# Attention weights of 20 pairs turned by VectorE and DMAs instead of TensorE, in a fused attention and feed-forward kernel

## The chip, the cores and the metric

One core of a Trainium2 chip runs the whole program in one launch. The metric is the device time of one execution in microseconds (us), as the median of several runs. TensorE is called PE (its matmuls) and PEld (its weight loads, which overlap the matmuls), VectorE is DVE, ScalarE is ACT, GpSimd is POOL and SyncE is SP. DMAs can be started from the queues of SP and of ACT.

## The reference

q, k and v are [8 batches, 8 heads, 576 positions, 64], all float32. For each of the 64 heads two attentions are computed and added:

- pooled: q, k and v are averaged over groups of 4 positions, which leaves 144; softmax attention over the 144, and each of the 144 results is repeated 4 times;
- local: softmax attention in which position i sees only the positions j with |i - j| < 4.

```
out_up    = repeat(softmax(q_d k_d^T / 8) v_d, 4)
out_local = softmax(where(|i-j| < 4, q k^T / 8, -1e9)) v
x = (out_up + out_local), heads side by side      # [4608 tokens, 512]
h = x @ w_in                                      # [4608, 2048]
g = h if h >= 1, 0 if h <= -1, else (h + 1)^2 / 4
out = g @ w_out                                   # [4608, 512]
```

## The kernel before

**Numbers in two parts.** The feed-forward products run in a float32 form of reduced precision (fp32r). Each operand is held as a high and a low part (`xh`, `xl` for x; `gh`, `gl` for g; two halves of each weight tile), and each product is the sum of three matmuls.

**Pairs, chunks, steps.** Two heads that lie side by side make a pair; there are 32 pairs, four to a batch. The tokens go through the feed-forward part in 11 chunks: one of 512, eight of 384, two of 512. In the first stage (the order written out in `ORDER`, lines 97 to 142) PE works on pairs 0 to 7 and on chunk 0. In the last stage the last two chunks go through a scheme with fewer products (`strassen`). Between them lies the middle stage, the loop of lines 1176 to 1216. Each of its steps n runs `mm1`, 12 matmuls of 384 columns that make one 128-row slice of h (line 858), and `mm2`, 9 matmuls of 512 columns that take up the slice of g from two steps before (line 921). Between the two, on ACT, DVE and POOL, lies the gate: ACT copies the slice out of its one PSUM bank (`m`, line 879), so that the next `mm1` can write there, DVE and ACT form g (lines 883 to 889), ACT rounds it (`gh`, 896), POOL takes the rest (`gl`, 902). At the end of each chunk ACT copies three output banks to `osb` (line 945), and SP's queue stores them (line 946).

**Joins.** The attention of pairs 8 to 31 is joined into the middle stage: `JOINS` (line 149) lists the 25 steps at which a join stands. The join of pair n does, right behind `mm1` of its step, the value products of pair n - 1 and the scores of pair n, in one stretch of small matmuls: the pooled values (line 633, which read the weights `ap`), the local scores in windows of 64 positions (651), the pooled scores (619), and last the local values (675, which read the weights `al`). Then DVE, POOL and ACT take maxima, exponentials and sums (lines 695 to 737), DVE adds up x of pair n - 1 (717), and `split` copies it to `xh` on ACT (581) and takes the rest to `xl` on POOL (582). In the next step DVE sums, inverts and multiplies (743 to 746 the local weights `sl`; 247 and 254, in `normalise`, the pooled weights `sp`, with a second copy `sp_rest` of the last 16 keys). The weights then lie with the queries on the partitions, and the value products need the keys there. From pair 10 on three DMAs of SP copy them to fresh tiles (759 to 762), so that they can be read as fp32r. One more step later PE turns them with 11 transposes of 128 by 128: five for the local weights (776), six for the pooled ones (779). ACT copies both out of PSUM to `ap` and `al` (784, 789). `al` is not needed before the end of the next join, which stands three to seven steps behind.

**What sets the order.** Each engine works through its own queue in a fixed order. A planner puts the instructions of the middle stage in order when the program is built; `tc.keep_in_program_order` ties PE's, `tc.issue_after(x)` puts a block's instructions behind x on x's engine, and `tc.high_priority` lets the gate go first. Tiles with one tag share one buffer: `x` and `ap` share one, `al` and `local` another, `vp` and `pooled` a third, and a writer waits until the readers of the tile before are done.

Of the kernel before, what the change touches and what calls it, by code (L numbers as in the profile page):

```python
# [10 lines left out]
F32 = mybir.dt.float32  # L11
# [35 lines left out]
WIN = 64  # L47
# [2 lines left out]
OUT_LEN = [61, 58, 58, 58, 53, 58, 58, 58, 58, 56]  # L50
NB = len(WIN_START)
NG = NB // 2

# [95 lines left out]
JOINS = [17, 20, 23, 26, 30, 37, 44, 51, 58, 63, 68, 73, 78, 85, 92, 99, 106, 111, 115, 120, 125]  # L149
JOINS += [131, 135, 138, 142]  # L150
assert len(JOINS) == NALL - SECOND + 1


class Rotation:
# [10 lines left out]
def attention_then_ffn(ctx: ExitStack, tc, qT, kT, vw, vp, vq, members, w_in, w_out, out):  # L165
# [24 lines left out]
    def load(n, name):  # L190

        if n == len(pairs):
            return
        b, p = pairs[n]
        if name in "qk" and n < NPAIR:
            t = wpool.tile([P, 1024], F32, name=f"first_{name}{n}", tag=f"w{'i' if name == 'q' else 'o'}{NFC - NPAIR + n}")
            source = (qT if name == "q" else kT)[b, p]
            queue = nc.scalar if name == "q" and n == 0 else nc.sync
            for c0, c1 in ((0, HALF), (HALF, S)) if n == 0 else ((0, S),):
                queue.dma_start(t[:, c0:c1], source[:, c0:c1])  # L200
        elif name in "qk":
# [395 lines left out]
    def pooled_sums(n):  # L597

        pooled_sum("q")
        pooled_sum("k")  # L600

    def join(n, pool):

        scores = pool.tile([P, 2, 512], F32, name="score_ps", tag="ga")
# [10 lines left out]
        def pooled_scores(i):  # L615
            for h in range(2):
                hs = slice(h * D, (h + 1) * D)
                x = h if i < 2 else 1 - h
                put(nc.tensor.matmul(
                    sp_v[i][x * D : (x + 1) * D, :],  # L620
                    state["qd"][hs, i * QB : i * QB + D],
                    state["kd"][hs, :],
                    start=True,
                    stop=True,
                    skip_group_check=True,
                ))

        def pooled_values(main):
            ap, vd = state["ap"], state["vd"]
            for h in range(2):  # L630
                hs = slice(h * D, (h + 1) * D)
                ks = slice(0, P) if main else slice((1 - h) * D, (2 - h) * D)
                put(nc.tensor.matmul(
                    pp_v[hs, :],
                    vd[ks, hs] if main else vd[ks, P : P + D],
                    ap[ks, 0 if main else 1, :, h, :],
                    start=main,
                    stop=not main,
                    skip_group_check=True,
                ))  # L640
# [3 lines left out]
        if n < NALL:  # L644
            q, k = loaded["q"], loaded["k"]
            for g in range(NG):
                for h, s in ((0, 0), (1, 1), (1, 0), (0, 1)):
                    x = h ^ s
                    w = WIN_START[x * NG + g]
                    hs = slice(h * D, (h + 1) * D)  # L650
                    put(nc.tensor.matmul(
                        sl_v[x * WIN : (x + 1) * WIN, s, g * WIN : (g + 1) * WIN],
                        q[hs, w : w + WIN],
                        k[hs, w : w + WIN],
                        start=True,
                        stop=True,
                        skip_group_check=True,
                    ))
            pooled_scores(0)
        if n > SECOND:  # L660
            pooled_values(False)
        if n < NALL:
            pooled_scores(2)
            pooled_scores(1)
        if n > SECOND:
            al, v = state["al"], loaded["v"]
            for g in range(NG):
                for r, h in ((0, 0), (1, 0), (0, 1), (1, 1)):
                    s = r ^ h
                    hs = slice(h * D, (h + 1) * D)  # L670
                    rs = slice(s * WIN, (s + 1) * WIN)
                    i = r * NG + g
                    o = OUT_START[i]
# [39 lines left out]
        if n > SECOND:  # L713
            x = apool.tile([P, S], F32, name="x", tag="ap", bufs=1)
            xd = apool.tile([P, SD], F32, name="xd", tag="kd", bufs=1)
            nc.vector.tensor_scalar_mul(xd, pp_v, 1.0 / FACTOR)
            nc.vector.tensor_tensor(
                x.rearrange("p (a s f) -> p a s f", a=2, f=FACTOR),
                pl_v.rearrange("p a (s f) -> p a s f", f=FACTOR),
                xd.rearrange("p (a s) -> p a s", a=2).unsqueeze(3).broadcast_to(  # L720
                    [P, 2, SD // 2, FACTOR]
                ),
                op=ALU.add,
            )
        if n == SECOND + 1:
            yield
        if n < NALL:
            nc.scalar.activation(slf, slf, AF.Exp, scale=0.125)  # L728
            for j, i in enumerate((0, 2, 1)):
# [5 lines left out]
                    scale=scale,  # L735
                    accum_out=sums[:, NB + i : NB + i + 1],
                )
        if n > SECOND:
            split(n - 1, x)
        if n == NALL:  # L740
            return
        yield
        nc.vector.tensor_reduce(sums[:, 0:NB], slf, axis=AX.X, op=ALU.add)
        nc.vector.tensor_scalar_add(scales, sums, 1e-9)
        nc.vector.reciprocal(scales, scales)
        nc.vector.tensor_tensor(
            slf, slf, scales[:, 0:NB].unsqueeze(2).broadcast_to([P, NB, WIN]), op=ALU.mult
        )
        normalised = normalise(sp, scales)
        vpt = loaded["vp"]  # L750
        vd = apool.tile([P, P + D], F32, name="vd", tag="vd", bufs=1)
        state["vd"] = vd
        with tc.issue_after(shifted.ins):
            nc.gpsimd.tensor_tensor(vpt[:, 0:2, :], vpt[:, 0:2, :], vpt[:, 2:4, :], op=ALU.add)
            nc.gpsimd.tensor_tensor(vd, vpt[:, 0, :], vpt[:, 1, :], op=ALU.add)
        moved = n > SECOND + 1
        if moved:
            local = apool.tile([P, NG * P], F32, name="local", tag="al", bufs=1)
# [175 lines left out]
    def result(c, t):  # L934

        osb = temp("osb", F32, "osb")
        rows = out[CHUNKS[c][0] : CHUNKS[c][0] + CHUNKS[c][1], :].rearrange("(a b) d -> b a d", a=2)
        rows = rows[t * P // 2 : (t + 1) * P // 2]
        if c == LATE + 1 and t == 2:
            nc.vector.tensor_copy(osb[:, 0:256], places["o"](t)[:, 0:256])  # L940
            nc.scalar.copy(osb[:, 256:], places["o"](t)[:, 256:])  # L941
            nc.sync.dma_start(rows[:, :, 0:256], osb[:, 0:256])
            nc.scalar.dma_start(rows[:, :, 256:], osb[:, 256:])
        else:
            nc.scalar.copy(osb, places["o"](t))  # L945
            nc.sync.dma_start(rows, osb)
        done("osb")

    def mm2(c, f):
# [368 lines left out]
```

## Time and profile before

| | |
|---|---|
| time, median of 3 runs | 886.82 us (886.55 to 886.97) |
| time of the profiled execution | 887.74 us |
| its span, from the first to the last instruction | 885.9 us |
| PE, PEld busy | 99%, 90% |
| DVE, ACT, POOL busy | 62%, 52%, 42% |
| granted TensorE clock | 1.000 of full speed |
| HBM, read and written | 101 GB/s over the span |

The profile is one execution. A row of the timeline gives the start and the duration of an instruction; PE's matmuls are pipelined, so that one starts long before the one in front of it has ended, and the pace is read from start to start. The float32 matmuls of the attention stand in the trace as two records each.

### The profile page before, as it was taken

What the parts mean: (1) busy time and instruction counts of PE and PEld (TensorE: products, weight loads), DVE (VectorE), ACT (ScalarE), POOL (GpSimd) and SP (SyncE); (2) the same over time, 40 slices, a digit from 0 to 9 for tenths busy, and PEclk for the clock granted to TensorE, in tenths of its full rate; (3) what the DMA queues carried; (4) which work ended last, traced back from release to release, by engine and by line L of the source; (5) the groups of instructions that cost most, each with busy time, mean ns of one, the idle gap of its engine ahead of it and who ended that gap; (6) DMA issues with size and microseconds to landing.
All of it is one profiled execution on the core that took longest, in us unless ns stands there. A gap on an engine that the chain in (4) does not pass through costs nothing. (4 is left out here: it accounts for less than half of the span.)

```text
span 885.9 us, 19654 instructions
## 1 busy us (share of the span) xinstructions
PE 876.9 (99%) x7766; PEld 794.0 (90%) x7766; DVE 548.3 (62%) x1062; ACT 460.0 (52%) x1015; POOL 370.3 (42%) x365
## 2 busy tenths in 40 slices
PE   8999999999999999999999999999999999999998
PEld 6888878999999899999999999999999989999997
DVE  7988775775566556566666566665546557744452
ACT  5988655555545445554544544554454544434332
POOL 4466573444324424444433343444434435433232
PEclk9999999999999999999999999999999999999999
DMA  8785223333333423333333233342223222334431
GB/s 320 252 302 183 67 74 108 100 129 111 102 97 95 134 80 107 125 117 116 129 101 104 97 109 105 109 155 92 94 97 105 87 84 76 115 96 143 120 117 50
DMA packets 68173, 106.44 MB, mean 120 GB/s; under 512 B 5713, under 2 KB 34129, under 8 KB 68081
## 3 DMA queue, kind: packets, MB, share of 16 engines
q1 hardware_dynamic: 67648, 104.76, 36.6%
q8 instruction: 61, 1.00, 0.5%
q10 hardware_dynamic: 432, 0.43, 0.1%
q14 instruction: 32, 0.25, 0.1%
HBM read 71.48 MB, written 17.83 MB: 101 GB/s over the span
## 5 line engine op out<-in xcount | busy, mean ns | idle before, releaser
L902 POOL TENSOR_TENSOR gl<-u,gh 128x384 fp32r<-128x384 f32 (+1 forms) x176 | 194.6, 1106 | 396.5 <-ACT gh L896 303.4
L921 PE MATMUL ffn_o<-w_o,gh 128*128 128x512 f32 x1152 | 346.7, 383 | 1.4 <-POOL w_o L837 1.4
L858 PE MATMUL ffn_h<-xh,w_i 128*128 128x384 f32 (+1 forms) x1184 | 301.2, 337 | 0.0
L921 PEld LDWEIGHTS ffn_o<-w_o,gh 128*128 128x128 f32 x1152 | 211.2, 189 | 26.5 <-POOL w_o L837 1.8
L858 PEld LDWEIGHTS ffn_h<-xh,w_i 128*128 128x128 f32 x1184 | 209.8, 189 | 13.1 <-ACT m L879 2.8
L921 PE MATMUL ffn_o<-w_o,gl 128*128 128x512 f32 x576 | 218.5, 379 | 0.0
L858 PE MATMUL ffn_h<-xl,w_i 128*128 128x384 f32 (+1 forms) x592 | 197.4, 333 | 0.0
L883 DVE TENSOR_SCALAR u<-m 128x384 f32<-128x384 f32 (+1 forms) x160 | 77.2, 483 | 138.9 <-ACT m L879 123.4
L889 DVE SCALAR_TENSOR_TENSOR u<-m,u 128x384 f32<-128x384 f32 (+1 forms) x160 | 107.9, 675 | 79.3 <-ACT u L886 79.3
L896 ACT CAST gh<-u 128x384 fp32r<-128x384 f32 (+1 forms) x176 | 95.3, 543 | 116.9 <-DVE u L889 116.4
L886 ACT ACTIVATE u<-u 128x384 f32<-128x384 f32 (+1 forms) x176 | 97.2, 553 | 110.2 <-DVE u L883 107.6
L921 PEld LDWEIGHTS ffn_o<-w_o,gl 128*128 128x128 f32 x576 | 109.0, 189 | 15.4 <-POOL gl L902 0.2
L858 PEld LDWEIGHTS ffn_h<-xl,w_i 128*128 128x128 f32 x592 | 112.0, 189 | 2.3
L879 ACT COPY m<-ffn_h 128x384 f32<-128x384 f32 (+1 forms) x132 | 63.8, 483 | 56.0 <-PE ffn_h L858 50.6
L728 ACT ACTIVATE sl<-sl 128x640 f32<-128x640 f32 x24 | 17.7, 739 | 54.9 <-POOL sl L702 54.9
L582 POOL TENSOR_TENSOR xl<-x,xh 128x576 fp32r<-128x576 f32 (+4 forms) x32 | 35.4, 1110 | 16.7 <-ACT xh L581 16.6
L959 DVE SCALAR_TENSOR_TENSOR sums<-sums 128x128 f32<-128x128 f32 (+1 forms) x72 | 33.1, 460 | 1.8
L702 POOL TENSOR_TENSOR sl<-sl,mxl 128x640 f32<-128x640 f32 x24 | 30.2, 1260 | 1.8 <-DVE mxl L701 1.8
L837 POOL TENSOR_TENSOR w_o<-m,w_o 128x512 fp32r<-128x512 f32 x16 | 22.3, 1400 | 18.7 <-ACT w_o L832 18.7
L1078 POOL TENSOR_TENSOR m<-both 128x256 f32<-128x256 f32 x14 | 10.2, 730 | 45.6 <-DVE both L1077 41.0
L1071 DVE TENSOR_TENSOR both<-ffn_h,both 128x256 f32<-128x256 f32 x14 | 5.9, 424 | 34.3 <-PE ffn_h L1052 29.8
L837 POOL TENSOR_TENSOR w_i<-m,w_i 128x512 fp32r<-128x512 f32 x16 | 21.7, 1359 | 13.0 <-ACT w_i L832 12.1
(180 smaller groups left out, 1151.9 us busy)
## 6 DMA issues: line engine op xcount, KB each, us to landing
xh<-kept SPq DMA_DIRECT2D x56, 256.0 KB, 3.4
v<-vw SPq DMA_DIRECT2D x29, 320.0 KB, 3.9
vq_sb<-vq SPq DMA_DIRECT2D x24, 384.0 KB, 3.1
out<-osb SPq DMA_DIRECT2D x35, 256.0 KB, 2.4
raw_i<-w_in SPq DMA_DIRECT2D x16, 512.0 KB, 5.6
raw_o<-w_out SPq DMA_DIRECT2D x16, 512.0 KB, 6.8
kept<-words SPq DMA_DIRECT2D x32, 256.0 KB, 2.6
k_sb<-kT SPq DMA_DIRECT2D x28, 288.0 KB, 4.1
```

The lines of the kernel that those rows point to most:

```text
L582: nc.gpsimd.tensor_tensor(xl[:, p, dst], x[:, part], xh[:, p, dst], op=ALU.subtract)
L702: shifted = nc.gpsimd.tensor_tensor(slf, slf, ml.unsqueeze(2).broadcast_to([P, NB, WIN]), op=ALU.subtract)
L837: engine.tensor_tensor(w[:, 1], raw[name, f, "m"], w[:, 0], op=ALU.subtract)
L858: ins = nc.tensor.matmul(htiles[c, f], wi[:, wt, cc * P : (cc + 1) * P], turns(xt[:, cc, ts]), start=(cc == 0 and xt is xh and wt == 0), s ...
L879: utiles["copied"] = nc.scalar.copy(m, h)
L883: nc.vector.tensor_scalar(utiles[c, f], m if c > 0 else h, -1.0, 1.0, op0=ALU.max, op1=ALU.add)
L886: nc.scalar.activation(u, u, AF.Square, scale=0.5)
L889: utiles["last"] = nc.vector.scalar_tensor_tensor(u, utiles["m"] if c > 0 else h, 1.0, u, op0=ALU.max, op1=ALU.min)
L896: nc.scalar.copy(gh, utiles[c, f])
L902: nc.gpsimd.tensor_tensor(gl, utiles.pop((c, f)), gh, op=ALU.subtract)
L921: ins = nc.tensor.matmul(o, gt[:, ts], turns(weights["o", f][:, wt, :]), start=f == 0 and n == 0, stop=f == NFC - 1 and n == 2,)
L959: return nc.vector.scalar_tensor_tensor(out, a, 1.0, b, op0=ALU.mult, op1=op)
```

## The change

For 20 of the 24 joined pairs (`TURNED`: pair 11 on, those whose next join is at least four steps away) the transposes, their PSUM tiles and the two copies by ACT are gone. DVE turns each 32 by 32 block where it lies. DMAs on SP's queue write the blocks to DRAM in their places, others read them back to `ap` and `al`. The pooled weights come first, then the local ones are multiplied and turned. The windows of these pairs start at other positions (`TURN_START`, `TURN_PARTS`), and the host lays v out for them; the local values of a pair take 22 matmuls in place of 20. The copy of x to `xh` and the rest to `xl` are queued behind the next step's copy of h, for the joins but the first two and the last. The stores of the results of chunks 1 to 8 go to ACT's queue. Chunk 0 and the last two keep theirs.

```diff
+TURN_START = WIN_START[: NG - 1] + [S // 2 - 61] + WIN_START[NG:]
+TURN_PARTS = [[(0, 32, 2)]] + [[(3, 29, 2)]] * (NB - 2) + [[(8, 24, 1), (32, 32, 1)]]
+TURNED = {SECOND + i for i in range(2, NALL - SECOND) if JOINS[i + 1] - JOINS[i] >= 4}
+    def turn_pooled(sp):
+        flat = apool.tile([P, 5, NQB, 32], F32, name="turned_sp", tag="vp", bufs=1)
+        nc.vector.transpose(flat[:, 0:4], sp[:, :, 0:P].rearrange("p i (k c) -> p k i c", c=32))
+        last = nc.vector.transpose(flat[:, 4], sp[:, :, SD - 32 : SD])
+        pooled = dram.tile([160, 2, 160], F32, name="pooled", tag="pooled", bufs=2)
+        for x in range(2):
+            for a in range(2):
+                rows = slice(x * WIN + a * 32, x * WIN + a * 32 + 32)
+                nc.sync.dma_start(
+                    pooled[:, x, a * WIN : (a + 1) * WIN].rearrange("(k c) f -> c k f", k=5),
+                    flat[rows, :, 0:2].rearrange("c k i f -> c k (i f)"),
+                )
+            nc.sync.dma_start(
+                pooled[:, 1 - x, P:].rearrange("(k c) f -> c k f", k=5), flat[rows, :, 2],
+            )
+        return pooled, last
+    def turn_local(sl, pooled):
+        al = apool.tile([P, NG * P], F32, name="al", tag="al", bufs=1)
+        nc.vector.transpose(
+            al.rearrange("p (b x c) -> p b x c", b=2, c=32), sl.rearrange("p g r (b c) -> p b (g r) c", c=32)
+        )
+        local = dram.tile([P, NG * P], F32, name="local", tag="local", bufs=2)
+        for x in range(2):
+            for a in range(2):
+                rows = slice(x * WIN + a * 32, x * WIN + a * 32 + 32)
+                nc.sync.dma_start(
+                    local[x * WIN : (x + 1) * WIN, a * 320 : (a + 1) * 320].rearrange("(b c) f -> c b f", b=2),
+                    al[rows].rearrange("c (b f) -> c b f", b=2),
+                )
+        ap = apool.tile([P, 3, 160], F32, name="ap", tag="ap", bufs=1)
+        nc.sync.dma_start(ap[:, 0:2], pooled[0:P])
+        for h in range(2):
+            nc.sync.dma_start(ap[(1 - h) * WIN : (2 - h) * WIN, 2], pooled[160 - WIN : 160, h])
+        nc.sync.dma_start(al, local)
+        state.update(al=al, ap=ap)
...
-        if n > SECOND:
+        if n in (SECOND + 1, NALL):
             split(n - 1, x)
         if n == NALL:
             return
         yield
+        if n > SECOND + 1:
+            with tc.issue_after(utiles["copied"].ins):
+                split(n - 1, x)
...
+        if n in TURNED:
+            every = scales[:, NB:].unsqueeze(2).broadcast_to([P, NQB, SD])
+            nc.vector.tensor_tensor(sp, sp, every, op=ALU.mult)
...
+        if n in TURNED:
+            pooled, last = turn_pooled(sp)
+            with tc.issue_after(last.ins):
+                normalised = nc.vector.tensor_tensor(
+                    slf, slf, scales[:, 0:NB].unsqueeze(2).broadcast_to([P, NB, WIN]), op=ALU.mult
+                )
+            turn_local(sl, pooled)
+            yield
+            load(n + 1, "vp")
...
+            return
...
-            nc.sync.dma_start(rows, osb)
+            (nc.scalar if 0 < c < LATE else nc.sync).dma_start(rows, osb)
```

## Rows read from the trace of the kernel before

**Rows 1.** The page, parts 1 and 2: busy us, share and count; granted clock by slice.

```profile
PE 876.9 (99%) x7766; PEld 794.0 (90%) x7766; DVE 548.3 (62%) x1062; ACT 460.0 (52%) x1015; POOL 370.3 (42%) x365
...
PEclk9999999999999999999999999999999999999999
```

**Rows 2.** Groups by line on PE, the transposes: count, busy us, mean ns.

```profile
L779 PE MATMUL turn_ps<-units,pooled 128*128 128x128 f32 x132 | 14.9, 249 | 0.0
L776 PE MATMUL local_ps<-units,local 128*128 128x128 f32 x110 | 11.9, 241 | 0.0
```

**Rows 3.** Timeline of PE around one turn: start us, duration us.

```profile
574.16 0.49 PE L858 MATMUL ffn_h<-xh,w_i 128*128 128x384 f32 x2
...
576.11 0.59 PE L921 MATMUL ffn_o<-w_o,gh 128*128 128x512 f32 x2
...
578.05 0.54 PE L776 MATMUL local_ps<-units,local 128*128 128x128 f32 x5
...
578.94 0.56 PE L858 MATMUL ffn_h<-xh,w_i 128*128 128x384 f32 x2
...
580.97 0.59 PE L921 MATMUL ffn_o<-w_o,gh 128*128 128x512 f32 x2
```

**Rows 4.** Timeline of PE, a join and the start of the next, four steps on.

```profile
566.01 0.47 PE L633 MATMUL value_ps<-ap,vd 128*64 128x144 f32 x4
566.41 0.81 PE L651 MATMUL score_ps<-k_sb,q_sb 64*64 64x64 f32 x40
...
567.53 0.75 PE L675 MATMUL value_ps<-al,v 64*64 64x61 f32 x40
568.22 0.70 PE L921 MATMUL ffn_o<-w_o,gh 128*128 128x512 f32 x2
...
584.95 0.47 PE L633 MATMUL value_ps<-ap,vd 128*64 128x144 f32 x4
```

**Rows 5.** Timeline of DVE behind that join.

```profile
573.16 0.25 DVE L745 RECIPROCAL score_ps<-score_ps 128x13 f32<-128x13 f32 x1
573.45 0.82 DVE L746 TENSOR_TENSOR sl<-sl,score_ps 128x640 f32<-128x640 f32 x1
574.19 0.25 DVE L247 TENSOR_TENSOR sp_rest<-sp,score_ps 128x96 f32<-128x96 f32 x1
574.35 0.55 DVE L254 TENSOR_TENSOR sp<-sp,score_ps 128x384 f32<-128x384 f32 x1
574.82 0.35 DVE L883 TENSOR_SCALAR u<-m 128x384 f32<-128x384 f32 x1
```

**Rows 6.** Timeline of SP's queue: a DMA's issue behind the join, and three stores.

```profile
575.73 0.64 SPq L762 DMA_DIRECT2D pooled<-sp_rest  x1
...
880.34 1.89 SPq L946 DMA_DIRECT2D out<-osb  x3
```

**Rows 7.** DMA issues by line: count, KB each, median us from issue to landing.

```profile
out<-osb SPq DMA_DIRECT2D x35, 256.0 KB, 2.4
...
q_sb<-qT SPq DMA_DIRECT2D x28, 288.0 KB, 3.2
local<-sl SPq DMA_DIRECT2D x22, 320.0 KB, 2.5
```

**Rows 8.** Timeline of ACT at the end of a chunk.

```profile
437.94 0.58 ACT L945 COPY osb<-ffn_o 128x512 f32<-128x512 f32 x1
439.18 0.48 ACT L879 COPY m<-ffn_h 128x384 f32<-128x384 f32 x1 [0.66 <-PE ffn_h L858]
```

**Rows 9.** Timeline of PE at the same place: the next write to h.

```profile
440.88 0.49 PE L858 MATMUL ffn_h<-xh,w_i 128*128 128x384 f32 x2
```

**Rows 10.** Timeline of the end: a store started by ACT.

```profile
882.54 0.64 ACTq L943 DMA_DIRECT2D out<-osb  x1
```

**Rows 11.** Timeline of POOL ahead of chunk 2.

```profile
213.05 1.41 POOL L582 TENSOR_TENSOR xl<-x,xh 128x576 fp32r<-128x576 f32 x1 [0.85 <-ACT xh L581]
```

**Rows 12.** Timeline of PE, the first step of chunk 2: its last products.

```profile
215.36 0.33 PE L858 MATMUL ffn_h<-xl,w_i 128*128 128x384 f32 x1
```

More of the change, by code (lines that the diff above doesn't have):

```diff
@@ L600, in pooled_sums, with turned_part @@
         pooled_sum("k")
+    def turned_part(al, rows, column, c0, size, count):
+        half = al[rows, (c0 // 32) * 320 + column * 32 + c0 % 32 :]
+        return bass.AP(half.tensor, half.offset, [half.ap[0], (320 - c0 % 32, count), (1, size)])
+    def turn_pooled(sp):
[33 more added lines that the diff above has]
+        state.update(al=al, ap=ap)
     def join(n, pool):
@@ L618, in pooled_scores @@
                 x = h if i < 2 else 1 - h
+                q0 = min(i * D, SD + D - QB - D) if n in TURNED else i * QB
+                qd = state["qd"][hs, q0 : q0 + D]
                 put(nc.tensor.matmul(
                     sp_v[i][x * D : (x + 1) * D, :],
-                    state["qd"][hs, i * QB : i * QB + D],
+                    qd,
                     state["kd"][hs, :],
@@ L635, in pooled_values @@
                     vd[ks, hs] if main else vd[ks, P : P + D],
-                    ap[ks, 0 if main else 1, :, h, :],
+                    ap[ks, h if main else 2, 0:SD] if n - 1 in TURNED else ap[ks, 0 if main else 1, :, h, :],
                     start=main,
@@ L648, in join @@
                     x = h ^ s
-                    w = WIN_START[x * NG + g]
+                    w = TURN_START[s * NG + g] if n in TURNED else WIN_START[x * NG + g]
                     hs = slice(h * D, (h + 1) * D)
@@ L664, in join @@
             pooled_scores(1)
-        if n > SECOND:
+        if n - 1 in TURNED:
+            al, v = state["al"], loaded["v"]
+            for g in range(NG):
+                for r, h in ((0, 0), (1, 0), (0, 1), (1, 1)):
+                    hs = slice(h * D, (h + 1) * D)
+                    s = r ^ h
+                    rs = slice(s * WIN, (s + 1) * WIN)
+                    i = r * NG + g
+                    for c0, size, count in TURN_PARTS[i]:
+                        o = TURN_START[i] + c0 - r * S // 2
+                        put(nc.tensor.matmul(
+                            pl_v[hs, r, o : o + size * count],
+                            v[rs, 2 * g + h, :],
+                            turned_part(al, rs, 2 * g + r, c0, size, count),
+                            start=r == 0,
+                            stop=True,
+                            skip_group_check=True,
+                        ))
+        elif n > SECOND:
             al, v = state["al"], loaded["v"]
@@ L715, in join @@
             xd = apool.tile([P, SD], F32, name="xd", tag="kd", bufs=1)
-            nc.vector.tensor_scalar_mul(xd, pp_v, 1.0 / FACTOR)
+            if n - 1 in TURNED:
+                there, here = xd[:, 0:P].rearrange("p (i b c) -> p b i c", b=2, i=2), pp_v[:, 0:P]
+                nc.vector.tensor_scalar_mul(there, here.rearrange("p (b i c) -> p b i c", b=2, i=2), 1.0 / FACTOR)
+                nc.vector.tensor_scalar_mul(xd[:, P:], pp_v[:, P:], 1.0 / FACTOR)
+            else:
+                nc.vector.tensor_scalar_mul(xd, pp_v, 1.0 / FACTOR)
             nc.vector.tensor_tensor(
@@ L737, in join @@
                 )
-        if n > SECOND:
+        if n in (SECOND + 1, NALL):
             split(n - 1, x)
@@ L745, in join @@
         nc.vector.reciprocal(scales, scales)
[L746 to L749, printed above, removed]
+        if n in TURNED:
+            every = scales[:, NB:].unsqueeze(2).broadcast_to([P, NQB, SD])
+            nc.vector.tensor_tensor(sp, sp, every, op=ALU.mult)
+        else:
+            nc.vector.tensor_tensor(
+                slf, slf, scales[:, 0:NB].unsqueeze(2).broadcast_to([P, NB, WIN]), op=ALU.mult
+            )
+            normalised = normalise(sp, scales)
         vpt = loaded["vp"]
@@ L755, in join @@
             nc.gpsimd.tensor_tensor(vd, vpt[:, 0, :], vpt[:, 1, :], op=ALU.add)
+        if n in TURNED:
+            pooled, last = turn_pooled(sp)
+            with tc.issue_after(last.ins):
+                normalised = nc.vector.tensor_tensor(
+                    slf, slf, scales[:, 0:NB].unsqueeze(2).broadcast_to([P, NB, WIN]), op=ALU.mult
+                )
+            turn_local(sl, pooled)
+            yield
+            load(n + 1, "vp")
+            if n + 1 < NALL:
+                with tc.issue_after(normalised.ins):
+                    pooled_sums(n + 1)
+            return
         moved = n > SECOND + 1
@@ L1264, in words, with cut @@
         return np.ascontiguousarray(a).view(np.int64)
-    windows = np.stack([v[:, :, w : w + WIN, :] for w in WIN_START], axis=2)
-    windows = windows.reshape(B, NPAIR, 2, 2, NG, WIN, D).transpose(0, 1, 3, 5, 4, 2, 6).copy()
+    def cut(starts):
+        windows = np.stack([v[:, :, w : w + WIN, :] for w in starts], axis=2)
+        return windows.reshape(B, NPAIR, 2, 2, NG, WIN, D).transpose(0, 1, 3, 5, 4, 2, 6).copy()
+    windows, turned = cut(WIN_START), cut(TURN_START)
     late = windows[SECOND // NPAIR :]
+    for n in TURNED:
+        windows[divmod(n, NPAIR)] = turned[divmod(n, NPAIR)]
     late[..., 1, :] = late[:, :, ::-1, ..., 1, :].copy()
@@ L1281 @@
         blocks[:, :, first : first + SD - P, :, 2] = late[:, :, P:, :, h]
+    for n in TURNED:
+        b, p = divmod(n - SECOND, NPAIR)
+        blocks[b, p, :, :, 2] = np.roll(blocks[b, p, :, :, 2], 3 * (SD - P), axis=0)
     pos = np.arange(WIN)
```

## The prediction

> **What bounds the kernel now.** I read the page's busy shares first. PE is busy for 876.9 of 885.9 us, and no slice of the span shows less than full granted clock (level 2.4 GHz) [rows 1]. Busy PE is not proof that PE is never waiting, as the ends of matmuls are modelled; so I went to PE's timeline and read the pace from start to start. A step without a join or a turn takes 574.16 to 578.05 = 3.89 us: 1.95 for the twelve products of h, 1.94 for the nine of the output [rows 3]. That is 1.95/12 = 0.16 us per 384 columns and 1.94/9 = 0.22 per 512, and the whole middle stage runs at this pace. So in this stage PE sets the end; what leaves PE's queue there is saved, and what makes PE wait is lost, one for one. DVE, ACT and POOL have room on average (62, 52, 42% [rows 1]); they matter only by a date that they miss.
>
> **The change part by part.**
>
> *The transposes go.* Each pair of the middle stage has eleven: 110 records of the local ones and 132 of the pooled ones are 22 times 5 and 6 [rows 2] (pairs 8 and 9 turn unmoved weights). In the timeline the eleven take from 578.05 to 578.94 = 0.89 us, and the twelve products behind them 2.03 us rather than 1.95 [rows 3]. So a turn costs 0.97 us, and 20 of them 19.4 us. Above or below: without the 0.08 it is 17.8.
>
> The mean durations of these rows, 249 and 241 ns, are latencies that overlap, not their price [rows 2]. The Trainium skill ("TensorE: Matmul & The Clock Gate", Part 4: PE-mode transpose) gives some 275 ns for a 128x128 transpose within a kernel; the duration here agrees nearly, but 220 x 0.275 = 60.5 us, an estimate by that page, would bring the execution to about 834 us. The starts 0.08 us apart rule that out, and it gets no chance.
>
> *Two more value matmuls per pair.* The local values take 0.69 us for 20 matmuls, 40 records (567.53 to 568.22 [rows 4]). 22 of them take 0.07 us more, 1.4 us over 20 pairs. That their moving operand now comes in two runs of 29 is not in any row; I bound it by 0 and by as much again, 2.8.
>
> *DVE's new work.* No transpose of DVE is in this trace. The nearest rows are DVE's operations over the same number of elements: 0.82 us for 640, 0.55 for 384, 0.25 for 96 [rows 5], 1.6 us together; half and double are my bounds. The one multiply of sp replaces two (0.25 + 0.55) and takes about 0.55 x 432/384 = 0.62. x's small term is split in two, at most 0.25 more. DVE gains some 1.7 us per pair, 34 us in all, and goes from 548 [rows 1] to about 580 us. It stays far from PE. What is queued behind it is the gate's u, and behind that ACT's square and the rest; but a slice of g is used only two steps, 7.8 us, after its h, so I cost this at nothing. ACT loses two PSUM copies per pair; PE does not wait for them, so that too is nothing.
>
> *The new round trip.* This is the part that can cost. For each turned pair SP issues 14 DMAs in place of 3: six pooled blocks to DRAM, four local ones, three loads of ap, one of al. I follow it from the start of a join (566.01 [rows 4]).
> - DVE's reciprocal ends at 573.41, +7.40 [rows 5]. Multiply 0.62, transposes 0.55 and 0.25: +8.82. The gate's u (0.35 [rows 5]) now comes sooner, as ACT copies h ahead of x; with it +9.17.
> - Stores are issued 1.89/3 = 0.63 us apart; a DMA between tiles 0.64 [rows 6]. Six from +9.2: the last starts at +12.35 and lands 2.4 later (a store lands in 2.4 [rows 7]), +14.75. The local weights are ready by then (9.17 + 0.82 + 0.82, one u2 more, under +11.5). Their four DMAs start at +13.0 to +14.9; the last lands at +17.3.
> - SP is free at +15.5 and loads ap: 160 KB, less than the 2.5 us of local and the 3.2 of q [rows 7], say 2.5: +18.0. The load of al waits for +17.3, then 320 KB in 3.2: +20.6.
>
> PE wants ap at the start of the next join and al 1.52 us later (567.53 - 566.01 [rows 4]). At a distance of four steps the next join starts at 584.95 - 566.01 = +18.94 today [rows 4], without the turn at +17.97. So ap comes just in time, and al (wanted at +19.49) is 1.1 us late. The distances of the 20 pairs, from the list of joins, are: four steps 4 times, five 7 times, six once, seven 8 times. With five (another 3.89: +21.9 and +23.4) both are early by 2.8 us and more. The last pair, one of those with four, is followed by a join without scores, so al is wanted up to 0.81 earlier (the 40 records of scores [rows 4]): 1.9 late. Sum: 3 x 1.1 + 1.9 = 5.2 us. Bounds: with transposes at half, u behind them and al loaded in the 2.5 us of local [rows 7], all is in time, 0. With DVE's new work doubled, and loads 1 us longer, each of the four waits 3 to 4 us and those with five steps up to 0.4, 18 us together. I take 5.2, the value of the nearest rows. Behind the waiting matmul stands all of PE, and nothing hides it. Behind SP's wait for the landing stand the load of the next pooled v and, at the next join, q and k; all have several us until they are used.
>
> *Stores on ACT.* A store started by ACT holds its queue 0.64 us [rows 10], and it must wait for the copy in front of it. Three at a chunk's end take 1.9 us and some 0.2 of waiting. ACT's copy of h ends there at 439.66 with 0.66 idle before it [rows 8], and PE writes the bank again at 440.88 [rows 9]. Room: 0.66 + 1.22 = 1.88, and ACT needs 2.1: 0.2 to 0.3 late if all three stand in front of the copy, 0 if the planner puts the copy, which has priority, ahead. Taken: 0.15 at each of eight chunk ends, 1.2 us; bounds 0 and 0.9 each, 7.
>
> *x behind the next h.* ACT copies h 0.67 us sooner behind a join. PE did not wait for it, so nothing is gained. What is late next is xl. Chunks 2 and 5 start two steps after the join that completes their tokens. There xl ends at 213.05 + 1.41 = 214.46, and the products that want it start at 215.36 [rows 11, 12]: 0.9 us of room, against a copy of 0.48 that goes in front [rows 8]. Nothing; if the square of u goes in front too, 0.1 to 0.6, twice.
>
> Sum against the profiled execution: 887.74 - 19.4 + 1.4 + 5.2 + 1.2 = 876.1 us. That execution lies 0.92 above the median of the runs, 886.82; so I forecast 875.2.
>
> **The rivals.**
>
> *No wait at all.* The round trip is in time at four steps as well and ACT's stores fit in. For it: ap misses by nothing in my chain and al by 1.1, less than the uncertainty of two DMA hops. Against: it needs both hops at the fast end. 887.74 - 19.4 + 1.4 = 869.7, on the median's level 868.8.
>
> *ACT becomes late at chunk ends.* Three waits and issues stand in front of the copy of h and of the gate, and the full 0.9 us is lost eight times: 7.2 in place of 1.2, 881.2. For it: room and need differ by only 0.2. Against: the gate's priority, and the copies that ACT no longer makes.
>
> *The round trip through DRAM is slow, and the kernel becomes slower.* The blocks go out in runs of 128 and 256 bytes. Place: PE's wait for ap and al at the next join. If the trip takes d us longer than I added up, pairs at four steps wait 1.1 + d (the last 1.9 + d), those at five from d = 2.8 on, those at six and seven not at all. The 16.8 us that are otherwise gained (19.4 - 1.4 - 1.2) are used up when 5.2 + 4d + 7(d - 2.8) = 16.8, at d = 2.85. With d = 4, two us more on each hop, the waits are 5.2 + 16 + 8.4 = 29.6 and the time 887.74 - 16.8 + 29.6 = 900.5, on the median's level 899.6. For it: no DMA with such short runs and such a landing is shown in my rows. Against: stores and copies of 256 to 320 KB land in 2.4 and 2.5 us whatever their direction [rows 7], and a block has 80 KB at most. The Trainium skill ("DMA: Bandwidth & Descriptors", Specifications) says that runs under 512 bytes fall short of full rate, since the DMA engine then reads, changes and writes back; by it the six pooled stores would land later. No row shows such a run; this rival's chance includes it.
>
> **How the numbers follow.** Forecast (870 to 880 of its own) 0.57; no wait 0.19; ACT late 0.13; slow round trip 0.11. 0.2% is 1.8 us, about what a measurement can tell from no change. The first three are all faster by far. Of the slow trip I give 0.08 to slower, 0.02 to a d near 2.85, which ends within 0.2%, and the rest to faster: faster 0.90, same 0.02, slower 0.08. The range goes from 868.0, just under no wait at all, to 884.0, which takes in late stores or a trip that is 2.2 us longer; about 0.12 is left above it and some 0.05 below.
>
> **What the changed profile would show.** 44 transposes of moved and unmoved pairs are left on PE (four pairs of eleven), and a turn's place in a step shows 3.89 us. The span of a join grows by 0.07. At joins four steps behind a turned pair PE's start of the local values comes about 1 us late, with a DMA into al as releaser; at five steps no wait. DVE shows three transposes per pair, about 1.6 us together. If PE waits at five steps, the slow trip is right. If PE's next h waits for ACT's copy at chunk ends, the second rival is. The forecast is wrong if a step without a join no longer takes 3.89 us, since then an engine other than PE sets the pace.

## The result and the profile after

The changed kernel takes 892.83 us (median of 6 runs, 890.55 to 895.57), the kernel before 886.89 (6 runs): ratio 1.0066, 95% interval 1.0043 to 1.0089. It is slower by 6 us, where 11.6 us less were forecast. The profiled execution took 895.22 us, with a span of 893.4 against 885.9.

The page after, parts 1 and 2, answers to [rows 1]:

```profile
PE 872.9 (98%) x7626; PEld 780.6 (87%) x7626; DVE 585.9 (66%) x1122; ACT 435.2 (49%) x975; POOL 369.1 (41%) x365
...
PEclk9999999999999999999999999999999999999999
```

PE now stands idle for 893.4 - 872.9 = 20.5 us; it was 885.9 - 876.9 = 9.0. DVE has 37.6 us more to do (34 forecast); 9.5 of them are the gate's own u, which takes 86.7 us in all where it took 77.2 (the page, part 5; the row stands with e13).

PE's timeline after, around a join without a wait (start us, duration us; it answers to [rows 3, 4]):

```profile
571.33 0.47 PE L684 MATMUL value_ps<-ap,vd 128*64 128x144 f32 x4
...
572.85 0.89 PE L726 MATMUL value_ps<-al,v 64*64 64x64 f32 x44
573.67 0.70 PE L1015 MATMUL ffn_o<-w_o,gh 128*128 128x512 f32 x2
...
575.72 0.49 PE L952 MATMUL ffn_h<-xh,w_i 128*128 128x384 f32 x2
...
577.67 0.59 PE L1015 MATMUL ffn_o<-w_o,gh 128*128 128x512 f32 x2
...
579.61 0.51 PE L952 MATMUL ffn_h<-xh,w_i 128*128 128x384 f32 x2
```

The turn is gone: from one h to the next 579.61 - 575.72 = 3.89 us. The join takes 573.67 - 571.33 = 2.34 us; before it took 568.22 - 566.01 = 2.21 [rows 4].

What PE and ACT wait for in the whole execution (us in total, times, longest); the one row of the kernel before stands first:

```profile
ACT m L879 <- PE ffn_h L858: 50.6, 49, 3.8
```
```profile
ACT m L973 <- PE ffn_h L952: 25.3, 25, 3.8
ACT m L973 <- DMA out<-osb: 8.4, 9, 2.9
PE ffn_h L952 <- ACT m L973: 7.8, 16, 2.1
PE value_ps L726 <- DMA al<-local: 3.4, 3, 2.5
...
PEld ffn_h L952 <- POOL xl L587: 0.3, 1, 0.3
```

Before, ACT waited 50.6 us for PE: the gate was early. Now half of that is left, and PE waits for ACT's copy of h in 16 places; the kernel before has no such wait. One of them, two steps behind a join at 268.7: DVE, ACT, POOL and PE (start, duration, in brackets the idle time before and what ended it). It answers to [rows 5].

```profile
277.12 0.60 DVE L825 TENSOR_TENSOR sp<-sp,score_ps 128x432 f32<-128x432 f32 x1
277.81 0.58 DVE L615 STREAM_TRANSPOSE turned_sp<-sp 128x384 f32<-128x384 f32 x1
278.31 0.86 DVE L977 TENSOR_SCALAR u<-m 128x384 f32<-128x384 f32 x1
279.09 0.27 DVE L616 STREAM_TRANSPOSE turned_sp<-sp 128x96 f32<-128x96 f32 x1
279.29 0.78 DVE L840 TENSOR_TENSOR sl<-sl,score_ps 128x640 f32<-128x640 f32 x1
279.99 0.53 DVE L983 SCALAR_TENSOR_TENSOR u<-m,u 128x384 f32<-128x384 f32 x1
```
```profile
276.48 0.48 ACT L973 COPY m<-ffn_h 128x384 f32<-128x384 f32 x1
276.84 0.78 ACT L586 CAST xh<-x 128x320 fp32r<-128x320 f32 x2
279.21 0.52 ACT L980 ACTIVATE u<-u 128x384 f32<-128x384 f32 x1 [1.59 <-DVE u L977]
280.56 0.51 ACT L990 CAST gh<-u 128x384 fp32r<-128x384 f32 x1 [0.83 <-DVE u L983]
280.98 0.47 ACT L973 COPY m<-ffn_h 128x384 f32<-128x384 f32 x1
```
```profile
277.39 1.56 POOL L587 TENSOR_TENSOR xl<-x,xh 128x320 fp32r<-128x320 f32 x2 [1.02 <-ACT xh L586]
```
```profile
281.50 0.59 PE L952 MATMUL ffn_h<-xh,w_i 128*128 128x384 f32 x2 [0.33 <-ACT m L973]
```

The copy of h is ready for DVE at 276.96, but u starts at 278.31, behind a multiply and a transpose, and takes 0.86 us with POOL's xl beside it; u's second operation comes behind another transpose and the multiply of sl. ACT's queue is in order: the gate's gh stands in front of the next copy of h. From copy to copy 280.98 - 276.48 = 4.50 us go by, more than the 3.89 of a step, and as there is one bank for h, PE waits. ACT's copy of x ends at 277.62; the square stands idle behind it for 1.59 us, until u is there.

Two longer waits of PE, and behind each the stretch in which the granted clock falls to half, 1.2 GHz (busy us of PE, PE's weight loads, DVE, ACT and POOL, then the clock, DMA share and GB/s):

```profile
224.92:227.02 2.10, 0.00 (x2) 0.00 (x1) 0.00 (x0) 0.48 (x1) 0.00 (x0) 1.00 0.62 241
228.50:231.90 3.40, 3.40 (x11) 2.93 (x10) 2.77 (x8) 1.75 (x4) 1.10 (x1) 0.50 0.00 1
593.01:595.51 2.50, 0.00 (x0) 0.00 (x1) 2.26 (x4) 0.51 (x1) 1.48 (x2) 1.00 0.93 319
597.10:600.50 3.40, 3.40 (x10) 2.81 (x10) 3.10 (x8) 1.31 (x6) 0.71 (x2) 0.50 0.37 101
```

The first wait is at a chunk's end, where the copy of h wants a tile that a store still reads (ACT; answers to [rows 8, 10]):

```profile
221.04 0.68 ACTq L1040 DMA_DIRECT2D out<-osb  x1
...
226.49 0.48 ACT L973 COPY m<-ffn_h 128x384 f32<-128x384 f32 x1 [2.87 <-DMA out<-osb]
```

The store issued at 221.04 lands 5.4 us later; before, a store took 2.4. The second wait is for al at a near join. The round trip's DMAs (count, KB each, median us to landing; answers to [rows 7]):

```profile
local<-al SPq DMA_DIRECT2D x80, 80.0 KB, 1.8
al<-local SPq DMA_DIRECT2D x20, 320.0 KB, 3.7
out<-osb ACTq DMA_DIRECT2D x24, 256.0 KB, 2.5
pooled<-turned_sp SPq DMA_DIRECT2D x80, 40.0 KB, 1.7
ap<-pooled SPq DMA_DIRECT2D x20, 160.0 KB, 2.3
...
pooled<-turned_sp SPq DMA_DIRECT2D x40, 20.0 KB, 1.5
```

### The profile page after: what moved, and what is told of

It reads as the page before. It is cut to its first block, busy times and chain, and to the rows that moved or that the text cites. A ratio compares the mean times of both kernels' runs of the same rounds, so it can differ in the third digit from the quotient of the medians.

```text
span 893.4 us, 19655 instructions
## 1 busy us (share of the span) xinstructions
PE 872.9 (98%) x7626; PEld 780.6 (87%) x7626; DVE 585.9 (66%) x1122; ACT 435.2 (49%) x975; POOL 369.1 (41%) x365
## 4 chain that ended last, share of the span: by engine, by line
PE 35%; DVE 22%; ACT 8%; DMA 6%; issue 3%; POOL 1%; SPq 1%; ACTq 0%; DVEq 0%; POOLq 0%
PE ffn_o L1015 16%; PE ffn_h L952 10%; PE ffn_h L1146 7%; DVE u L977 4%; DVE u L983 4%; DVE sums L1053 3%; ACT u L980 2%; DMA out<-osb 2%; ACT sp L804 2%; DMA kept<-words 2%; ACT m L973 1%; DVE x L791 1%; DVE al L633 1%; DMA k_sb<-kT 1%; DVE sp L825 1%
## 5 line engine op out<-in xcount | busy, mean ns | idle before, releaser
L977 DVE TENSOR_SCALAR u<-m 128x384 f32<-128x384 f32 (+1 forms) x160 | 86.7, 542 | 108.7 <-ACT m L973 87.6
```

The lines of the kernel that those rows point to most:

```text
L977: nc.vector.tensor_scalar(utiles[c, f], m if c > 0 else h, -1.0, 1.0, op0=ALU.max, op1=ALU.add)
```

## The experiments

Each was timed in five rounds against the kernel before on the same chip (887.0 to 887.5 us). The theory at the start: the loss sits in SP's and ACT's queues at chunk ends and in al. The rival, which took over: the gate is late, because of what stands ahead of it on DVE and ACT.

**The change's parts, one by one.** Stores back on SP (e1), x back at its old place (e2), both (e3: the turn alone).

```diff
-            (nc.scalar if 0 < c < LATE else nc.sync).dma_start(rows, osb)
+            nc.sync.dma_start(rows, osb)                      # e1, e3
-        if n in (SECOND + 1, NALL):
+        if n > SECOND:                                        # e2, e3
             split(n - 1, x)
-        if n > SECOND + 1:
-            with tc.issue_after(utiles["copied"].ins):
-                split(n - 1, x)
```

> Only the stores of chunks 1 to 8 go back to SP's queue. Theory A (ScalarE's own queue makes its copy of h late at chunk ends: three waits and issues there, and h's copy waits for a store's landing because it reuses that store's tile): the 8.5 us that PE loses at chunk ends and one slow-clock stretch of 1.7 us mostly go, 883 to 886 us. Theory B (the turn's DMAs make landings slow and fill SP's queue; the issuing engine does not matter): the chunk ends stay as they are or get worse, 892 to 898 us.

> Only the copy of x to xh and its rest xl go back to their old place, ahead of the next h. Theory A (xl on GpSimd now falls on VectorE's first gate operation u, which takes 0.9 us instead of 0.35 beside it, and everything behind is late by 0.5): the 0.2 to 0.6 us that PE loses in the second step behind a turned join, 7 us in all, go for the most part, 886 to 889 us. Theory B (u and u2 are late because the transposes stand ahead of them in VectorE's queue, with or without xl): within 1.5 us of the changed kernel, 891 to 894 us.

> The turn by VectorE and DMAs alone: stores on SP's queue and x in its old place. If both side edits cost what theory A says, the gains add up: 876 to 881 us, faster than before. If the turn itself is the cause (VectorE's queue, DMA load): 888 to 897 us.

Measured: e1 900.15 us (1.0149, 1.0132 to 1.0165), e2 883.44 (0.9959, 0.9944 to 0.9974), e3 892.18 (1.005, 1.0036 to 1.0064). e1 lost more than theory B allowed, e2 gained more than theory A. So with the turn the stores on ACT save 7.3 to 8.7 us, against what I had expected; e1's trace has 18.3 us of ACT waiting for stores where the changed kernel has 8.4. And the move of x costs 8.0 to 9.4 us. The turn alone (e3) is 5 us slower than the kernel before.

The two side edits each alone on the kernel before:

> The kernel before with one edit alone: results of the middle chunks stored by ScalarE's queue; weights are still turned on PE. Theory A (the stores on ACT pay only because the turn fills SP's queue and the DMA engines; PE of the kernel before waits less than 2 us in all in the joined stage, so nothing is there to win): 886 to 889 us. Rival B (the edits' effects add: turn with and without it differ by 8.8 us, so it saves 7 to 9 here too): 878 to 881 us.

> The kernel before with one edit alone: ACT's copy of x, and POOL's small part of it, behind the next copy of h. Theory A (the move puts POOL's small part beside the gate's u two steps behind a join, and the 0.9 us turn on PE there hides it): 887 to 891 us. Rival B (the edits' effects add: with the turn gone the move costs 8 to 9 us): 894 to 897 us.

Measured: e6 888.16 us (1.0009, 1.0 to 1.0017), e7 887.93 (1.0007, 0.9998 to 1.0016): nothing, either way. Both effects exist only once the turn has left PE.

**Which half of the move of x.** ACT's copy xh at its old place, only POOL's xl queued behind the copy of h:

```diff
-        if n in (SECOND + 1, NALL):
-            split(n - 1, x)
+        if n > SECOND:
+            split(n - 1, x, "hl" if n in (SECOND + 1, NALL) else "h")
...
-                split(n - 1, x)
+                split(n - 1, x, "l")
```

> The changed kernel with ACT's copy of x back at its old place, in front of the copy of h, and only POOL's small part left where the change put it, behind the copy of h. Theory A (what costs 9 us in the move is ACT's order: the copy of x stands ahead of the gate's square): 882 to 885 us. Rival B (it is POOL's small part running beside the gate's u, which then takes 0.9 us in place of 0.35): 890 to 893 us.

Measured: 883.60 us (0.9966, 0.9952 to 0.9979), the same as e2. It looks like theory A, but the trace shows that the edit did not move xl: in e13 POOL starts it right behind ACT's copy of x, ahead of u, as it does in e2. POOL, ACT and DVE in e13:

```profile
272.82 1.55 POOL L589 TENSOR_TENSOR xl<-x,xh 128x320 fp32r<-128x320 f32 x2 [0.64 <-ACT xh L587]
```
```profile
272.94 0.49 ACT L975 COPY m<-ffn_h 128x384 f32<-128x384 f32 x1
```
```profile
274.12 0.47 DVE L979 TENSOR_SCALAR u<-m 128x384 f32<-128x384 f32 x1
```

All u of the changed kernel and of e13 (count, busy us, mean ns, idle us before):

```profile
L977 DVE TENSOR_SCALAR u<-m 128x384 f32<-128x384 f32 (+1 forms) x160 | 86.7, 542 | 108.7 <-ACT m L973 87.6
```
```profile
L979 DVE TENSOR_SCALAR u<-m 128x384 f32<-128x384 f32 (+1 forms) x160 | 77.3, 483 | 107.3 <-ACT m L975 84.7
```

So e13 is e2 over again and does not tell the halves apart. The traces speak for rival B. In the changed kernel the square stands right behind the copy of x in 22 places of the middle stage, and in 21 of them it waits 1.5 to 1.8 us for u: the copy of x is not in its way. Counted from the start of a join (medians over 19 joins), u starts at +9.06 us in the changed kernel and at +8.96 in e2, but takes 0.92 and 0.54 us, and the copy of h behind that gate starts at +12.05 and +11.30. ACT's order matters in that a late copy of x makes xl late, and xl then runs beside u. Over the whole kernel u costs 9.9 us more than in e2 (76.8), and the move costs 9.4. No run keeps x behind h and xl away from u, so this stays a reading of traces.

**Fewer pairs: only those with five steps or more.** e4 with all edits, e8 with x at its old place.

```diff
-TURNED = {... if JOINS[i + 1] - JOINS[i] >= 4}
+TURNED = {... if JOINS[i + 1] - JOINS[i] >= 5}
```

> The turn only for the 16 pairs whose next join is at least five steps away, both side edits kept. The waits for al at the four near joins (4.7 us in the trace, and a slow-clock stretch of 1.7 us behind the longest) go and four turns of 0.97 us come back on PE: 889 to 891 us. If the near joins cost nothing in untraced runs: 896 us.

> The changed kernel with x copied at its old place, and only the 16 pairs at least five steps before the next join turned by VectorE. Against the 20-pair version of it (883.4 us): four turns come back on PE (+3.9), their eight more value matmuls go (-0.6). Theory A (near joins wait some 4 us for al, with 1.7 us of slow clock behind the longest wait): 880 to 883 us. Rival B (the al waits are hidden by other waits anyway): 885 to 888 us.

Measured: e4 890.83 us (1.0036, 1.0023 to 1.0049), e8 882.55 (0.9946, 0.9934 to 0.9958). The four near pairs cost about as much as their turns on PE; most of the loss is elsewhere.

**The next pooled v loaded behind al** (e9), and **sums of weights a step earlier** (e12; DVE adds up weight tiles in the middle stage and SP stores the sums): two tries to free landings.

```diff
+            with tc.issue_after(back.ins):       # e9: back is the load of al
                 load(n + 1, "vp")
-SUMS = [..., 75, 82, 88, 89, 95, 102, 103, 108]
+SUMS = [..., 75, 81, 88, 89, 95, 101, 102, 108]  # e12, on e8
```

> The changed kernel with x copied at its old place, and the load of the next pooled v (384 KB) put behind the load of al on SP's queue; it went between ap and al. Theory A (al lands late because this load is ahead of it and shares the DMA engines): the wait of 2.7 us at the near join and the slow clock behind it shrink or go, 878 to 882 us. Rival B (al is late by the earlier hop, or waits are dominated by chunk ends): 882 to 885 us, as without this edit (883.4).

> The version with 16 turned pairs and x copied at its old place (882.6 us), with three of the sums of weights a step earlier (step 82 to 81, and 102, 103 to 101, 102), so that their stores are not followed at once by the loads of q, k and v at joins 85 and 106. Theory A (these stores land in 4.3 us in place of 2.6 since the join now comes 1 us sooner and its loads share the DMA engines; the gate's u wants their tile): two waits of 0.8 to 1.0 us go, 880 to 882 us. Rival B (another wait takes their place): 882 to 884 us.

Measured: e9 884.23 us (0.9961, 0.9949 to 0.9973), e12 883.90 (0.9963, 0.9952 to 0.9975): no gain. In e9 the wait for al went from 2.7 to 0.9 us, but PE's waits for the copy of h rose from 5.6 to 8.6. In e12 the two waits shrank (0.76 to 0.39, 1.00 to none), while one of 1.18 became 2.57 and one of 0.84 came new. One wait takes the place of another; what they share, as I read it, is a gate without room.

**VectorE's transposes.** e10 leaves them out; e14 does them, but the blocks do not wait for them; e15 leaves them out with x behind h.

```diff
-        flat = apool.tile([P, 5, NQB, 32], F32, name="turned_sp", tag="vp", bufs=1)
-        nc.vector.transpose(flat[:, 0:4], ...)
-        last = nc.vector.transpose(flat[:, 4], ...)
+        flat = sp.rearrange("p i c -> p (i c)")
...
-        nc.vector.transpose(al..., sl...)
+        flat = sl.rearrange("p g r c -> p (g r c)")
```

> The changed kernel with x copied at its old place, without VectorE's three transposes: the same blocks, in runs of the same length, go to DRAM straight from the unturned weights, so the products use unturned weights; all else, DMAs and value matmuls too, stays. By the order of SP's queue the next pooled v is also loaded behind al, which alone gave 884.2 us. Theory A (the transposes, 1.7 us per pair, stand ahead of the gate's u on DVE, and ACT's next copy of h waits for that gate): the waits for the copy of h one and two steps behind joins go, 877 to 880 us. Rival B (ACT's own queue and the landings set these waits): 882 to 885 us.

> The version without transposes (873.4 us), with the three transposes back at their place on VectorE, but the DMAs still read the unturned weights, so the blocks do not wait for them. Theory A (VectorE's time ahead of the gate is what costs): 881 to 885 us, as with turned weights. Rival B (the blocks leave DVE later, so loads and stores land together at chunk ends): 872 to 876 us.

> The changed kernel with all its edits, x behind the next h among them, but without VectorE's three transposes: the blocks go to DRAM unturned and the products use unturned weights. Theory A (the move of x costs only because the gate is late already, which it is only with the transposes): 873 to 877 us. Rival B (the move costs 8 to 9 us once the turn has left PE, whatever DVE does): 881 to 884 us.

Measured: e10 873.41 us (0.984, 0.9828 to 0.9853), e14 883.23 (0.9953, 0.9939 to 0.9966), e15 876.15 (0.9873, 0.986 to 0.9886). Waits in e10, then in e14 (the views as above):

```profile
ACT m L965 <- PE ffn_h L944: 43.6, 58, 3.8
...
PE ffn_h L944 <- ACT m L965: 1.3, 3, 0.5
```
```profile
ACT m L972 <- PE ffn_h L951: 24.4, 31, 3.8
...
PE ffn_h L951 <- ACT m L972: 6.5, 10, 2.2
```

All three fell on theory A's side, e10 lower than either range. Without the transposes the kernel is 10 us faster where x has its old place (883.4 against 873.4), and 892.8 - 876.2 = 16.7 us where x is moved. Without the transposes the move costs 2.7 us in place of 9.4. Later blocks are not the reason: in e14 the blocks start as early behind a join as in e10 (+8.4 and +8.2 us for the pooled ones, +11.2 and +11.1 for the local ones), and all of the gain is lost.

One more thing differs, which I had wrong in what I expected of e10. The tile `turned_sp` shares its buffer with the next pooled v, so with the transposes that load waits until the pooled blocks are out. Without them it goes ahead of the blocks, not behind al. SP's queue in e10 (join at 233.9), then in e14 (join at 236.3):

```profile
240.64 0.33 SPq L214 DMA_DIRECT2D vq_sb<-vq  x1
...
248.53 0.44 SPq L644 DMA_DIRECT2D al<-local  x1
```
```profile
250.79 0.59 SPq L214 DMA_DIRECT2D vq_sb<-vq  x1
251.58 0.33 SPq L650 DMA_DIRECT2D al<-local  x1
```

So the 10 and the 16.7 us are the worth of the transposes and of the later load of v together, and no run separates them. Step by step from PE's starts, 1.8 of the 9.2 us between the traces of e14 and e10 stand at the first chunk's end, where in e14 this load and al run beside a store.

**Relief for the gate.** u on ACT in the two steps behind a turned join (e16); the transposes behind the gate on DVE (e11, 16 pairs).

```diff
+            if state.get("near"):                                        # e16
+                nc.scalar.activation(utiles[c, f], m, AF.Relu, bias=1.0)
...
-            pooled, last = turn_pooled(sp)
+            with tc.issue_after(utiles["last"].ins):                     # e11, on e8
+                pooled, last = turn_pooled(sp)
```

> The changed kernel with x copied at its old place, and the gate's u of the two steps behind a turned join made by ACT (a Relu of h + 1, 0.5 us, in the 1.2 us that ACT waits there for DVE's u) in place of DVE, where it is queued behind the transposes. Theory A (the queue in front of u on DVE makes the gate late): 875 to 880 us against 883.4. Rival B (the gate's second operation stands behind the same work on DVE, so nothing is won): 882 to 885 us.

> The version with 16 turned pairs and x copied at its old place (882.6 us), with the transposes queued behind both of the gate's operations on DVE (u and its second one) of the step behind the join. The pooled blocks leave some 1 us later, for which pairs with five steps have 2.8 us of room. Theory A (the order on DVE makes the gate late): 878 to 881 us. Rival B (DVE's order is not what delays the copy of h): 882 to 884 us.

Measured: e16 877.85 us (0.9897, 0.9878 to 0.9917), e11 888.94 (1.0019, 1.001 to 1.0028). In e16 ACT no longer hands u to DVE and back (ACT, behind the join at 270.1):

```profile
277.87 0.50 ACT L970 COPY m<-ffn_h 128x384 f32<-128x384 f32 x1
278.39 0.52 ACT L972 ACTIVATE u<-m 128x384 f32<-128x384 f32 x1
278.95 0.52 ACT L979 ACTIVATE u<-u 128x384 f32<-128x384 f32 x1
281.15 0.52 ACT L989 CAST gh<-u 128x384 fp32r<-128x384 f32 x1 [1.68 <-DVE u L982]
281.57 0.47 ACT L970 COPY m<-ffn_h 128x384 f32<-128x384 f32 x1
```

Copy to copy is 3.70 us, under a step. e16 keeps the transposes and the order of the DMAs and gains 5.6 us over e2 (e18 below 5.7 over e8): this much is the gate's, whatever the later load of v costs. e11 went against both theories: PE waits 9.3 us for copies of h in e11's trace (4.8 in e8's). Two things are new there: the last transpose stands ahead of the next step's u, and the u ahead of the transposes now runs beside xl for longer, so that all u take 87.5 us (78.6 in e8). Which of the two weighs more I have not told apart. Landings are not it: a store takes up to 4.6 us in e11, up to 5.3 in e8.

**The turn on PE as cover.** Three idle operations on DVE in the kernel before (e17):

```diff
         if moved:
+            tails = sp_rest.rearrange("p i (x c) -> p i x c", x=2)[:, :, :, 0 : SD - P]
+            for part in (sp[:, :, 0:P], tails, slf):
+                nc.vector.tensor_tensor(part, part, part, op=ALU.max)
```

> The kernel before with three idle operations more per pair on VectorE, behind the weights' scaling and in front of the moves, over 384, 96 and 640 elements (some 1.6 us, about the transposes' time); they change no value. Theory A (the 0.97 us turn on PE gives the gate room, so that the same work on DVE is hidden): 887 to 890 us. Rival B (DVE's work costs the gate as much with the turn on PE): 895 to 899 us.

Measured: 940.88 us (1.0606, 1.0591 to 1.0622). Both theories missed, and the run does not answer its question: these operations also delay the moves, and PE stands idle in front of each of the 22 turns (19 times with this releaser). One such row; the move of the local weights that it turns was issued at 252.11 and landed at 254.61:

```profile
254.74 0.58 PE L779 MATMUL local_ps<-units,local 128*128 128x128 f32 x5 [1.61 <-DVE u L892]
```

The kernel before had no room between a pair's moves and its turn. That the turn gave the gate room rests on other runs: the move of x costs nothing with the turn on PE (e7), and 2.7 us without turn and transposes (e15 against e10). It was the smaller part. ACT's wait for PE is 50.6 us before, still 43.6 in e10 with the turn gone, and 24.4 in e14 with the transposes and the later load of v.

**The best version.** e16 with 16 pairs (e18), and e16 with u on ACT in the join's own step too (e19, `for d in (0, 1, 2)`).

> The version with x at its old place and the gate's u on ACT in the two steps behind a turned join (877.9 us), with only the 16 pairs turned that are at least five steps before the next join. Four turns and their copies come back (+3.9), eight value matmuls go (-0.6); the wait of 1.7 us for al at the near join and, where it comes, a longer wait at the first chunk's end behind a near join go. Theory A: 875 to 878 us. Rival B (the near joins cost less than their turns): 878 to 881 us.

> The same version with 20 turned pairs, with u on ACT in the join's own step as well. Theory A (the gate comes into the join 0.4 us earlier, so DVE starts the joined scores earlier): 875 to 878 us. Rival B (ACT, not DVE, is what is late there): 878 to 881 us.

Measured: e18 876.88 us (0.9881, 0.9866 to 0.9896), e19 877.63 (0.9887, 0.987 to 0.9905). e18 beats both kernels; e19 is no better than e16.

## Why the prediction was wrong

*The turns, -19.4: right.* The turn is gone from every turned pair, and where PE does not wait the step shows 3.89 us. Many steps behind joins and at chunk ends show more, the sign that I had named for an engine other than PE setting the pace.

*The value matmuls, +1.4: mis-sized.* A join takes 0.13 us more, not 0.07; times 20 that is 2.6, near my upper bound of 2.8.

*DVE's new work, "nothing": this step failed.* The durations were right (means 0.58, 0.26 and 0.83 us against 0.55, 0.25 and 0.82). The date was wrong. I gave the gate 7.8 us, until its slice of g is used. But ACT's queue is in order: gh, which ends the gate, stands ahead of the next copy of h, and with one bank of h PE needs that copy one step later. Taking u out of DVE's queue, with the transposes left in, gives 5.6 us (e16). Leaving the transposes out, and with them the hold on the next pooled v, is worth 16.7 us with everything else in place (e15), nearly the whole distance from 875.2 to 892.8. That e15's 876.15 us lies so near the forecast is in part luck: its waits for al are 1.3 us, not 5.2, while the move of x costs 2.7 there and the value matmuls 1.2 more than I had put.

*x behind the next h, "nothing": failed with it.* Undoing it gives 9.4 us (e2). I priced the ACT time that the move sets free and xl at chunks 2 and 5 (0.3 us, once, right), not that xl would run beside the gate's u and stretch it (0.92 us against 0.54), which is what the traces show in the place of my "nothing". In the kernel before the same stretch costs nothing (e7: all u 85.4 us, time as before), as the gate has room there; so this term hangs on the one above.

*The round trip, +5.2: about right in size.* (Its own sum is a little high: 17.3 + 3.2 is 20.5, not 20.6, and the four waits then add up to 4.8.) PE waits 3.4 us for al, at three near joins, with 1.7 us of half clock behind the longest. Taking the four near pairs out gains 0.9 to 2.0 us (e4, e8, e18) although it brings 3.3 us of turns back, so their waits, with what hangs on them, are worth 4 to 5 us. Of the slow round trip nothing showed: the blocks of 128- and 256-byte runs landed in 1.5 and 1.7 us, those of local, in runs of 1280 bytes and twice as large, in 1.8. By the rule of the Trainium skill on runs under 512 bytes ("DMA: Bandwidth & Descriptors", Specifications) they fall short of full rate; if that costs time here, it is too little to make them land later than the larger blocks of local.

*Stores on ACT, +1.2: wrong sign.* With the turn in SP's queue they save 7 us (e1). The waits at chunk ends that I feared from ACT did come: PE's steps at six chunk ends are 8.5 us longer than before. But the traces put them down to landings and to the gate, not to ACT's issues. The store above takes 5.4 us, while vq (384 KB, issued at 220.76) and al (320 KB, 221.45) load beside it; and with u on ACT alone the same six steps shrink by 2.5 us (e18 against e8). In e10, with neither the transposes nor that load beside the store, all of PE's waits for the copy of h are 1.3 us.

*The clock, not in the sum.* Two stretches of 3.4 us at 1.2 GHz, some 1.5 us behind PE waits of 2.1 and 2.5 us, cost 1.7 us each in the profiled execution (mean granted clock 0.996; the six executions have 0.996 to 0.999).

My rivals held no gate that DVE makes late: the second put the chunk ends' loss on ACT's issues, and the one that ended slower put the loss in DMA landings at the joins, where PE waited 3.4 us.

## What to carry to other kernels

A piece of work on the bounding engine can be part of the room in which another engine's loop catches up, and work that moves to that other engine takes more of it: before such a move, see how long the in-order loop behind it (here copy of h, u, square, u2, gh, next copy) takes against the step that is left, and who waited for whom by how much. An operation's deadline is that of the next instruction behind it in any in-order queue on its way, not that of the data it makes. A run meant to tell two causes apart should be read in its trace first, to see that it moved what it was to move: e13 left xl where it was, and e10 moved a load as well. Side edits that measure nothing by themselves should be timed again with the main edit in place: here one saved 7 us and the other cost 9.

## What the runs showed that I had not expected

A wait of PE can be followed by 3.4 us at half clock, but the wait's length alone does not decide: in e14 PE stood still for 2.22 us at the same chunk's end, and the clock stayed full.

```profile
224.17:226.39 2.22, 0.00 (x1) 0.00 (x1) 0.00 (x0) 0.48 (x1) 0.00 (x0) 1.00 0.06 21
226.39:232.00 5.61, 5.61 (x31) 5.37 (x32) 4.03 (x10) 2.56 (x5) 1.11 (x1) 1.00 0.12 47
```

DVE's u over 384 columns takes 0.35 us alone [rows 5] and 0.86 us in the changed kernel's timeline above, where POOL's xl runs beside it. Of the 160 u in that trace, none without an operation of POOL beside it took more than 0.43 us, over 384 or 512 columns.
